# Two of 192 attention tiles change from transposed ("upright") to ordinary scores, about 120 single operations change engine, and the order table is replaced

## The chip, the cores and the metric

The kernel runs on one NeuronCore of one Trainium2 chip. The metric is the device time of one execution in microseconds. TensorE is called PE here (its weight loads PEld), VectorE DVE, ScalarE ACT, GpSimd POOL and SyncE SP; all DMAs of this kernel are issued by SP.

## The reference

Clustered attention, then a softplus feed-forward network:

```python
q_assign = argmax(einsum('bhsd,hcd->bhsc', q_n, c_n), axis=-1)   # 16 centroids per head
k_assign = argmax(einsum('bhsd,hcd->bhsc', k_n, c_n), axis=-1)
mask   = q_assign[:, :, :, None] == k_assign[:, :, None, :]
scores = where(mask, scale * (q @ k.T), -1e9)
attn   = softmax(scores, axis=-1)
x      = (attn @ v).transpose(0, 2, 1, 3).reshape(3072, 512)
out    = softplus(x @ w_in) @ w_out          # w_in 512x2048, w_out 2048x512
```

Batch 4, 8 heads, 768 positions, head width 64. Inputs and output are float32 (the two weights arrive as 64-bit words and are converted on the chip); the kernel splits each operand into a high and a low float16 part, so that a product is two or three float16 matmuls.

## The kernel before

**Tiles and passes.** A tile t is 128 queries of one head. There are 8 passes (4 batches, two halves of the 768 queries each); a pass has 8 heads and 3 tiles per head, so 24 tiles. Tiles 0 to 23 are the first pass, 24 to 47 the second; both belong to batch 0 and use the same keys. Two neighbouring tiles make a pair: pair 17 is tiles 34 and 35.

**The two ways to compute scores.** An ordinary tile (`scores`, L971 to L1041) has 4 matmuls (L991) that give 128 queries by 768 keys, a row maximum on DVE (L1007), the exponential on ACT into `p` (L1013), a float16 copy of `p` on ACT (L1022), the rest `p` minus copy on POOL (L1024), both into `phl`, and, once for a pair, a DMA transpose of 24 blocks (`flip`, L303) from `phl` into `pt`, which the second product needs with keys on the partitions. Its second product (`attend`, L1071 to L1073) is 18 float16 matmuls. An upright tile (`upright`, L880 to L969) avoids the transposition: 2 matmuls (L890) for the maximum alone, the maximum on DVE (L902), a PE transpose of it (L909), a copy into an extra row of the queries on ACT (L915), then 12 matmuls (L926, L927) that give the scores already transposed with the maximum subtracted, and the exponential on ACT (L967). Its second product is done in float32 (L1067). The constant `UPRIGHT` lists the upright pairs: 0 to 17, so tiles 0 to 35. For heads with an upright tile, row 64 of the transposed keys is filled by a small DMA (`lift`, L529), and `prep_q` fills row 64 of those query tiles that are not upright by another (L770).

**Around them.** `prep_k`, `prep_q` and `prep_v` load keys, queries and values, split them and transpose them (on PE for the first heads, else by DMA); `nearest` (L533 to L587) finds the centroid of each row with small matmuls and a chain of DVE operations; `prep_weights` converts 32 pieces of the weights (L398 to L408). `ffn1` (L1138 to L1140), `softplus` (L1159 to L1187; its high part is `gh` by an ACT cast L1186, its low part a POOL subtraction L1187) and `ffn2` (L1216 to L1218) compute the network for one pass while the attention of the next is under way. All this overlaps: PE alternates between pieces of `ffn1` and `ffn2` and the attention tiles.

**What sets the order.** Each of these functions is a generator that yields one operation at a time, and the string `PLAN` says whose turn is next, two characters an entry. So each engine's instructions stand in the order that the table gives, and each engine runs its own in that order. An operation has an engine and a planned duration; where the table's planned times leave a gap on PE, `warm` (L273) puts filler matmuls there (L279), which compute nothing. SP's queue is in order as well: a DMA whose source is not ready holds up those behind it.

The lines that decide which pair is upright:

```python
UPRIGHT = (0, 1, ..., 17)                      # L33, shortened here
def is_up(t): return t // 2 in UPRIGHT         # L418
lows = [c for c in range(c12) if not is_up(at + c)]   # prep_q, L765
```

Of the kernel before, what the change touches and what calls it, by code (L numbers as in the profile page):

```python
# [12 lines left out]
AF = mybir.ActivationFunctionType  # L13
# [18 lines left out]
UPRIGHT = (0, 1, 2, 3, 4, 5, 6, 7, 8, 9, 10, 11, 12, 13, 14, 15, 16, 17)  # L32
# [3 lines left out]
QLO_POOL = (1, 4)  # L36
QT1_ACT = (0,)
POOLED = ('q0_0_0', 'q0_0_1')
SPLIT = ()
HI_POOL = ()  # L40
HALVES = (0,)

# [4 lines left out]
    "020306000704d1c3d2000000000000000000000001d3050501d40c0a000006060101d50101d1d106d1d2d2d606d1d2d2010101010101"  # L47
    "d70ac40507c305c4c50a070cd806d7d1d1d1d101d9d2d2d106d2d206d206d1d106d106d2d206d106c601da06dcd1dad2d2080bc70cdb"
    "d101c5d1d1070906c4061fc51fd2d21h1h1f1f08070808d2d21h1h1j1j1f0b0b1fc80b1j1l1l1h1h1j0ac3c4c5c31g1n1j1l1n1i0909"
    "09c51l1j0cc30a0c0509c3080808081p1p1k1n1n1l1l080808c9ca08cb1p1r1r0b0b0bdddd1n1n0b1pc61r1t1r1mc71t0b09090b1t1p"  # L50
    "1o09090bdfc4090909dfdh1p1r1r1tc8c4c51v1vdhdhdh1q1q1q1q1x1t1v1t1q1v1sc9didididjdedi1q1x1z1z1v1x1v1x1uccdg0bcd"
    "1z1z1x21c6c6c7c7c6c61w211z21ca1x23c7c8cac8c71zcb21cc1y23252321caca2120dk0dce1qcf2525c923cdc8cbc9c9cc27272225"
    "2222222323cac8c92927272222250d25292b2b242d272b2926ce27290d0dcdce2d2d292f28ccccce2b292f2hcbcb2f0d2b2d2f2bcccb"
    "2h2j2h2a2dcf2hce2d2ccgcg2f2e0d0d0d0d0dcdcf0dcf0d2j0d2l2jcg2f2ncfcf22chchcicjcd2j2e2e2e2g0d0d0d0d2l2h2h2n2lcg"
    "cg2j2j2n2ichch2n2lci2ech2p2pcgck2kce2l2l2pcicicichclci2n2r2r2pcj2ncjcj2m2t2p0e2rckckck2p2rckcj2ecm2ecjcd2o2r"
    "2r2t2v2v2q2q2q2q2tclcl2t2x2t2v0e0e0e2v2t2qck2q2s2v2x2x2v2xcm2z2z2ucn2q2x312zclclcmcmcmcm312w2z2xcl0e0e0eco2z"
    "33330e0e0e0e0e31312y2zcncncn33310f31cz353533czcpcococo0e33dncncndndn3735cz300f0f37czcq33coco35dodo3732390f0e"
    "0e0e0ecz35cr0hdododocpcq39cz323232323234320e3735dqdq0f3937363b3937cpcpcqcp39cr0fcqcqdqcz3b3b0fcpcrcr393b0f3d"
    "3dczcrcrcsdrdrdr0f0f38cz3b0h0h0f0fdrdr3bcq3d3dczdtdtdt3d0i3d3f3f3aczdsctcscscs3f3h3h3f3fdscz3c3j3j3e0fcscs0g"
    "0i0i3hd03ldud03hctct3jcz3n3hducu0i3e3e3e3h0jduct3l3j3e3eduducz0ict3lcu0gct3ndw3n3pd03rcudw0g0k0gcu3jdwczcz0i"  # L60
    "3p0i0icz3gcz3lcucucv3l3l3n3n3p3tdxdx3rdxcz3pdxdx3p3t3r3v3vd03i3pcz0jdycvcv0icv3tdydy3xcz0kdzd03kcz3m0jcvcvcw"
    "e03r3re03t3t3te03x3v3ze1e1e1e1e00ke03z3x3ocz3q3q3q3q0i0icwcw3zcxczczd0cz410k0ne2e23q0i0i0mcwcw3qe2e2czd0czcw"
    "e241d03x3v3ve3e3e3e4cxcx3x3x3se5e5e5e5cz3ue40gcxcx410ne5cxcze7e70n0n41413z3z0me6d00k0ke70k0k0k0k0k0kd0czd0cz"
    "e9e9e9e9cy3wd0ea0m413q3e0le8e83y0g0g0g0ge9cycy0gcy0gcy0g0g0g0gcy0gd0d0d04042420o42424242d0eb0g0o0l420n0n0n0n"
    "0nd0d00n0n0necec0keb0nd0434343430l0lcz43454545454545cz4747474747edcz4949494949ed49d0eeeeczef4b4b4bedd04d4dd0"
    "0l4fefef4def0oefd04f4b4b4h0l0l0l4h0l4d4d44d0egeg4f4j0l0l0l4jcz464d4h4l4l4hcz4f4f4h48cz4a4hczeh0l0l0l4jeheh4n"
    "4n4lcz4p0p0lcz4ceieiei4n4pcz4e4e4e4e4j4j4l4l4lejeieiejej4pczd0cz4g4e4e4eek4n4nekekcz0p4p4pelekekel4r4r4r4i4p"
    "4t4tczd0elel4t4v4v4r4r4k4x4x4t4t4m4t4vcz4x4z4zczemem514zcz4o0p0p4v4v51emem534q4q4q4qen4x4x4xencz51d0534q4q55"
    "55em4sen534z4zczeo514u5757eoeo0p5551514qczd0eoeo0p0p0pep57cz53534w59590p5555d04y55eqeqeq5b59cz5d0q5b0p0p0p0p"
    "0p0p5057575bczerer52520p0p5d595959er52525252ererczd0czesesesd0545b5b5d525d5dcz565dczetet0q5f5fetcz5f5h5hetcz"  # L70
    "5j0q0q5f5f5h5h5h5j5jcz58cz5a5h5l5ld0eweueueueu5jet5j5c5n5n5l5l5l5e5l5e5e5e5n5e5e5ed05p5p5p0r0qevevd05r0q0q0q"
    "0q0q0q0q5revd05t5g5n5n5t0q0qevd0ex5i5p5p5p5r5v5v5t5r0q0q5r5t5t5v5k5x5x5xcz5m5tczeyey0r0r5z5z5z5vczd0czezey5o"
    "5v5x5xezevcz61615q5qez5q5q0r616363czf0f0f0d05x65655scz5z5z0r5ucz0t0uezez5q63676161610r0rd06569f1f1f1f15w0r67"
    "0rcz69656563635y65czf1d067f2f20u0u0u0sf2cz696b6b0r0t0t5qczf4f4f4f36d0w6dcz67676b60czf5f5f569696262626962cz6f"
    "6fcz0r0r0r6b6b64czf6f6f6f6f66d0s0s0sf36d6d666d6fd0czf4f46hf7f76h6hf8f86h6hd00u0u0u0ud06j6j6jf868d0f9f90u0u0u"
    "6f6fcz6a6hcz0w0w6l6lfafafa62d06l0u0ufafa625q626n6n6nczfbfb6j6j6pczfcfcfc6l6l6ccz6e6e6e6pczfdfd6ed00s0s0s0s0s"
# [1238 lines left out]
```

## Time and profile before

| | us |
|---|---|
| median of 3 runs | 828.7 (827.96 to 829.2) |
| the profiled execution | 827.06 |
| its span in the profile | 825.2 |
| PE busy | 810.4 (98%) |
| ACT, POOL, DVE busy | 556.0, 507.6, 478.4 |
| clock granted to PE | full speed in each of the 40 slices |

The span runs from the first to the last instruction of the program; 1.86 us of the profiled execution lie outside of it. The profiled execution is 1.64 us under the median of the timed ones. Durations in the profile that belong to one matmul are longer than the time it keeps PE, since matmuls overlap: what one costs is read from the start of one to the start of the next.

### The profile page before, as it was taken

Reading aid. Unit: us, or ns where it says so; the run is one execution under the profiler, and the core shown is the slowest. Engines: PE = TensorE matmul, PEld = TensorE weight load, DVE = VectorE, ACT = ScalarE, POOL = GpSimd, SP = SyncE. Lnnn points to the kernel's source line nnn. Section 1 sums busy time; section 2 is a strip of 40 time slices with the busy share of each in tenths; the row PEclk is TensorE's granted clock in tenths of the full one; section 3 lists DMA queues with packets and bytes.
Section 4 is the critical chain, followed back from the end, with each engine's and each line's share of the span. In section 5 each row is a group of like instructions: output and inputs, shape, how many; then the busy total and the mean of one; then the engine's idle time right before and its main releaser. Section 6 shows DMA issues by size and latency. Waiting matters only on the chain.

```text
span 825.2 us, 19179 instructions
## 1 busy us (share of the span) xinstructions
PE 810.4 (98%) x7941; PEld 526.8 (64%) x7941; DVE 478.4 (58%) x861; ACT 556.0 (67%) x858; POOL 507.6 (62%) x361
## 2 busy tenths in 40 slices
PE   8899999999999999999999999999999999999998
PEld 8899886655666666656666666566666655655554
DVE  7788787676655856665674546667555453322111
ACT  6687788865787788658678677767767666623230
POOL 4743457884788778767686685756775656621210
PEclk9999999999999999999999999999999999999999
DMA  9987759999999999989989999999898776620001
GB/s 251 221 193 161 190 157 212 204 212 188 185 181 174 186 214 193 209 181 176 187 166 183 177 182 180 212 199 186 154 155 169 136 129 122 114 64 13 26 1 39
DMA packets 389815, 133.68 MB, mean 162 GB/s; under 512 B 367072, under 2 KB 382688, under 8 KB 389728
## 3 DMA queue, kind: packets, MB, share of 16 engines
q1 hardware_dynamic: 389728, 132.46, 80.7%
q8 instruction: 62, 1.02, 0.5%
q14 instruction: 25, 0.20, 0.1%
HBM read 35.68 MB, written 6.29 MB: 51 GB/s over the span
## 4 chain that ended last, share of the span: by engine, by line
PE 63%; issue 8%; DMA 5%; ACT 2%; DVE 2%; POOL 2%; POOLq 0%; DVEq 0%; ACTq 0%
PE s L991 10%; PE h L1138 7%; PE h L1139 7%; PE h L1140 7%; PE o L1218 7%; PE o L1216 7%; PE o L1217 7%; DMA pt<-phl 5%; PE mbank L1071 3%; PE mbank L1073 3%; PE mbank L1072 3%; POOL gh L1187 1%; ACT p L1013 1%; ACT phl L1022 0%; DVE fg L1171 0%
## 5 line engine op out<-in xcount | busy, mean ns | idle before, releaser
L1024 POOL TENSOR_TENSOR phl<-p,phl 128x768 f16<-128x768 f32 x156 | 255.9, 1652 | 114.0 <-ACT phl L1022 77.4
L1007 DVE TENSOR_REDUCE negm<-s 128x1 f32<-128x768 f32 x156 | 148.7, 954 | 91.6 <-PE s L991 89.9
L1013 ACT ACTIVATE p<-s,negm 128x768 f32<-128x768 f32 x156 | 139.4, 896 | 52.3 <-DVE negm L1007 46.8
L1138 PE MATMUL h<-xT,wi 128*128 128x384 f16 x512 | 166.7, 325 | 1.1 <-DVE fg L1171 1.1
L1140 PE MATMUL h<-xT,wi 128*128 128x384 f16 x512 | 166.8, 326 | 0.0
L1139 PE MATMUL h<-xT,wi 128*128 128x384 f16 x512 | 166.7, 326 | 0.0
L1187 POOL TENSOR_TENSOR gh<-fg,gh 128x768 f16<-128x768 f32 x64 | 105.2, 1646 | 86.9 <-ACT gh L1186 86.6
L1216 PE MATMUL o<-wo,gh 128*128 128x512 f16 x376 | 142.4, 379 | 0.4 <-DVE ot L1261 0.4
L1218 PE MATMUL o<-wo,gh 128*128 128x512 f16 x376 | 142.5, 379 | 0.0
L1217 PE MATMUL o<-wo,gh 128*128 128x512 f16 x376 | 142.4, 379 | 0.0
L1022 ACT CAST phl<-p 128x768 f16<-128x768 f32 x156 | 127.3, 828 | 19.7 <-DMA pt<-phl 17.5
L1171 DVE SCALAR_TENSOR_TENSOR fg<-fa,h 128x384 f32<-128x384 f32 x128 | 70.3, 550 | 119.7 <-ACT fa L1160 108.8
L1159 ACT ACTIVATE fa<-h 128x384 f32<-128x384 f32 x128 | 62.4, 487 | 111.2 <-PE h L1140 111.1
L991 PE MATMUL s<-kt,qt 128*128 128x384 f16 x624 | 126.9, 326 | 0.1
L1071 PE MATMUL mbank<-vb,pt 128*128 128x65 f16 x936 | 101.2, 192 | 3.0 <-DMA pt<-phl 3.0
L1072 PE MATMUL mbank<-vb,pt 128*128 128x64 f16 x936 | 101.3, 192 | 0.0
L1073 PE MATMUL mbank<-vb,pt 128*128 128x65 f16 x936 | 100.9, 194 | 0.0
L1071 PEld LDWEIGHTS <-pt 128*128 128x128 f16 x936 | 86.9, 98 | 17.0 <-DMA pt<-phl 5.1
L1072 PEld LDWEIGHTS <-pt 128*128 128x128 f16 x936 | 86.3, 97 | 11.6
L1073 PEld LDWEIGHTS <-pt 128*128 128x128 f16 x936 | 86.5, 97 | 0.0
L991 PEld LDWEIGHTS <-qt 128*128 128x128 f16 x624 | 57.6, 98 | 38.2 <-issue 0.6
L1140 PEld LDWEIGHTS <-wi 128*128 128x128 f16 x512 | 50.0, 98 | 33.2
(164 smaller groups left out, 1279.4 us busy)
## 6 DMA issues: line engine op xcount, KB each, us to landing
wo<-in_moe_w_in_dram SPq DMA_DIRECT2D x16, 512.0 KB, 6.0
wo<-in_moe_w_out_dram SPq DMA_DIRECT2D x14, 512.0 KB, 4.5
out_dram<-ot SPq DMA_DIRECT2D x23, 256.0 KB, 3.0
rawk<-in_k_dram SPq DMA_DIRECT2D x15, 384.0 KB, 4.2
rawq<-in_q_dram SPq DMA_DIRECT2D x15, 384.0 KB, 4.1
rawv<-in_v_dram SPq DMA_DIRECT2D x12, 384.0 KB, 4.5
rawv<-in_v_dram SPq DMA_DIRECT2D x8, 192.0 KB, 6.0
pt<-phl SPq DMA_TRANSPOSE x78, 6.1
```

What stands on the lines that cost most here:

```text
L991: nc.tensor.matmul(st[:, j, :SH], qt[:, s, i], kt[:, s, NT // 2 * j : NT // 2 * (j + 1)], start=(s == 0), stop=(s == 1),)
L1007: yield op("DVE", 950, lambda: nc.vector.tensor_reduce(negm, st[:, :, :SH], AX.XY, ALU.max, negate=True))
L1024: "POOL", 1640, lambda: nc.gpsimd.tensor_tensor(phl[:, u, 1], p32, phl[:, u, 0], ALU.subtract), shared=True
L1071: nc.tensor.matmul(av, pt[:, 0, c], vb[:, c, D : 2 * D + 1], start=(c == 0), stop=False)
L1072: nc.tensor.matmul(av[:, :D], pt[:, 0, c], vb[:, c, :D], start=False, stop=False)
L1073: nc.tensor.matmul(av, pt[:, 1, c], vb[:, c, D : 2 * D + 1], start=False, stop=(c == NT - 1))
L1138: nc.tensor.matmul(hp, w[0], x[0], start=(c == 0), stop=False)
L1139: nc.tensor.matmul(hp, w[0], x[1], start=False, stop=False)
L1140: nc.tensor.matmul(hp, w[1], x[0], start=False, stop=(c == NP - 1))
L1216: nc.tensor.matmul(po, g[0], wo[:, f, 0, 0], start=(f == f0), stop=False)
L1217: nc.tensor.matmul(po, g[0], wo[:, f, 0, 1], start=False, stop=False)
L1218: nc.tensor.matmul(po, g[1], wo[:, f, 0, 0], start=False, stop=(f == f0 + NF // 2 - 1))
```

## The change

`UPRIGHT` loses its last entry, 17. Tiles 34 and 35 are then ordinary. `prep_q` for heads 0 to 3 of the second pass gets a small DMA that fills row 64 of these two query tiles.

A new tuple `SWAPPED` names single operations that run on the other of two engines. Each such place in the code now has two engines with a planned duration for each:

```diff
+    def either(key, first, second, emit, **opt):
+        now, other = (second, first) if key in SWAPPED else (first, second)
+        if "shared" not in opt or now[0] == "ACT":
+            opt["shared"] = now[0] == "POOL"
+        return op(now[0], now[1], lambda: emit(engines[now[0]]), alt=other, key=key, **opt)
+    def cast(key, ns, slow, dst, src):
...
+        return either(key, ("ACT", ns), ("POOL", slow), emit)
...
-UPRIGHT = (0, 1, 2, 3, 4, 5, 6, 7, 8, 9, 10, 11, 12, 13, 14, 15, 16, 17)
+UPRIGHT = (0, 1, 2, 3, 4, 5, 6, 7, 8, 9, 10, 11, 12, 13, 14, 15, 16)
...
-        yield op("ACT", 830, lambda: nc.scalar.copy(phl[:, u, 0], p32))
-        yield op(
-            "POOL", 1640, lambda: nc.gpsimd.tensor_tensor(phl[:, u, 1], p32, phl[:, u, 0], ALU.subtract), shared=True
+        yield cast(f"ph{t}", 830, 1290, phl[:, u, 0], p32)
+        yield either(
+            f"p{t}",
+            ("POOL", 1640),
+            ("DVE", 950),
+            lambda e: e.tensor_tensor(phl[:, u, 1], p32, phl[:, u, 0], ALU.subtract),
+            shared=True,
...
-        eng, n_e, e = last
-        yield op(eng, n_e, lambda: e.tensor_scalar(other, sim, 1.0, MASK, ALU.subtract, ALU.mult), **here)
+        def mark(e):
+            if e is nc.scalar:
+                e.activation(other, sim, AF.Copy, bias=-MASK, scale=MASK)
+            else:
+                e.tensor_scalar(other, sim, 1.0, MASK, ALU.subtract, ALU.mult)
+
+        yield either(f"zk{n}", last[:2], ("ACT", 310), mark, **here)
```

Counted in `SWAPPED`, by kind:

- POOL to DVE: 23 subtractions of attention tiles (`p34, p35, p37, p39, p40, p41, p43, p45, p46, p61, p62, p64, p67, p82, p84, p85, p88, p90, p100, p102, p133, p190, p191`), 13 of the network (`g0_6, g0_7, g1_1, g1_7, g2_2, g2_5, g2_7, g6_5, g7_2` and `g7_4` to `g7_7`), 5 of the weights, 5 of `x`, 3 of keys (`k4, k8, k16`), 3 of values (`v8, v16, v20`), and 4 products of the later queries (`m`).
- ACT to POOL: 40 float32 to float16 copies: 12 of attention tiles (`ph`), 10 of the weights, 8 of the network, 7 of `x`, 2 of keys, 1 of values.
- DVE to ACT: 9 marks of key clusters (`zk`), 4 of query clusters (`zq`).
- ACT to DVE: 5 copies of the maximum (`u1, u12, u17, u22, u23`).
- At the start: the copies out of PSUM `kT0_0_0` and `qT1_0` go from ACT to DVE, `kT0_2_1`, `kT1_0_1`, `kT1_2_1` and `qT1_1` from DVE to ACT; the product `m0_0_0` goes from DVE to POOL and `m0_0_1` from POOL to DVE; the second half of the first keys' subtraction (`k0_1`) goes from DVE to POOL.

`PLAN` is replaced. Both tables have 3304 entries: `scores` of tile 34 has 5 instead of 6, `prep_q` of heads 0 to 3 in the second pass 18 instead of 17. Read as PE's order, the table after has the same phases in the same order, with neighbours exchanged; the scores of tiles 34 and 35 come between `ffn1` pieces 2 and 4 of the first pass, and the DMA transpose of this pair between weight loads 25 and 26. The first query load stands behind the first weight load instead of ahead of it, and the fill of row 64 of the first keys stands 13th on SP's queue instead of 16th. From `ffn1` piece 15 of the seventh pass to the end PE's order is the same in both.

Two waits (`acc`) are made explicit in `store` and `last_store`; they name what the order gave before.

## Rows read from the trace of the kernel before

**Rows 1.** The page's span and its first part: busy time, share of the span and instructions of each engine.

```profile
span 825.2 us, 19179 instructions
PE 810.4 (98%) x7941; PEld 526.8 (64%) x7941; DVE 478.4 (58%) x861; ACT 556.0 (67%) x858; POOL 507.6 (62%) x361
```

**Rows 2.** Busy time by stretch. Columns: the stretch and its length in us, then busy us and instructions of each engine, the clock granted to PE as a share of full speed, the busy share of the DMA engines, GB/s.

```profile
0.00:20.00 20.00, 17.20 (x298) 16.09 (x299) 14.29 (x66) 12.12 (x20) 8.81 (x23) 1.00 0.93 250
20.00:100.00 80.00, 76.02 (x917) 70.53 (x914) 66.10 (x118) 60.15 (x106) 40.61 (x38) 1.00 0.80 188
100.00:200.00 100.00, 97.20 (x913) 65.63 (x910) 75.17 (x130) 73.78 (x120) 67.48 (x50) 1.00 0.94 201
200.00:700.00 500.00, 498.01 (x5029) 307.74 (x5028) 294.74 (x499) 367.16 (x542) 359.56 (x233) 1.00 0.94 176
700.00:826.00 126.00, 121.96 (x798) 66.84 (x796) 28.06 (x49) 42.76 (x73) 31.13 (x20) 1.00 0.19 44
```

**Rows 3.** The filler matmuls of L279 alone, by stretch, in the same columns (PE and PEld only).

```profile
0.00:20.00 20.00, 10.78 (x153) 10.03 (x154) 1.00 0.93 250
20.00:100.00 80.00, 4.40 (x66) 3.71 (x62) 1.00 0.80 188
100.00:200.00 100.00, 0.53 (x7) 0.46 (x7) 1.00 0.94 201
```

**Rows 4.** PE's waits over the whole span: who waited for what, us in total, times, longest. These are three of eleven lines.

```profile
PE mbank L1071 <- DMA pt<-phl: 3.0, 4, 1.2
PE turned L909 <- ACT qt L915: 1.2, 1, 1.2
PE h L1138 <- DVE fg L1171: 1.1, 2, 0.6
```

**Rows 5.** PE's timeline around an upright tile: start, duration (of several, from the first start to the last end), instruction. The 12 of L926 and L927 run from 28.08 to 28.75.

```profile
26.41 1.50 PE L1067 MATMUL mbank<-rawv,ptf 128*128 128x65 f32 x12
27.75 0.49 PE L890 MATMUL m<-kt,qt 128*128 128x384 f16 x2
28.08 0.22 PE L926 MATMUL u<-qt,kt 128*128 128x128 f16 x1
...
28.75 0.28 PE L909 MATMUL turned<-eye,negu 128*65 128x128 f32 x1
28.86 0.33 PE L1067 MATMUL mbank<-rawv,ptf 128*128 128x65 f32 x2
```

**Rows 6.** PE's timeline around ordinary tiles: the 4 of L991 and what starts behind them; then the first of the 18 matmuls of a second product, and what starts behind the last of them.

```profile
210.15 0.81 PE L991 MATMUL s<-kt,qt 128*128 128x384 f16 x4
210.80 0.19 PE L1071 MATMUL mbank<-vb,pt 128*128 128x65 f16 x1
...
214.27 0.19 PE L1071 MATMUL mbank<-vb,pt 128*128 128x65 f16 x1
...
214.82 0.81 PE L991 MATMUL s<-kt,qt 128*128 128x384 f16 x4
```

**Rows 7.** SP's timeline: the stretch from 123.80, where the table after puts the new transpose, and the last attention transpose of the second pass.

```profile
123.80 0.47 SPq L298 DMA_DIRECT2D wo<-in_moe_w_out_dram  x1
127.00 2.15 SPq L303 DMA_TRANSPOSE kt<-kn  x1
...
130.78 0.50 SPq L298 DMA_DIRECT2D wo<-in_moe_w_out_dram  x1
134.60 1.43 SPq L303 DMA_TRANSPOSE kt<-kn  x1
...
180.62 4.76 SPq L303 DMA_TRANSPOSE pt<-phl  x1
```

**Rows 8.** PE's timeline, the longest wait in 183 to 198 us (in brackets: idle time before, and what ended it), and the piece of the critical chain (start, duration, what) that ends at it.

```profile
188.87 0.20 PE L1071 MATMUL mbank<-vb,pt 128*128 128x65 f16 x1 [1.16 <-DMA pt<-phl]
...
180.62 8.20 DMA pt<-phl
```

**Rows 9.** DVE's timeline just ahead of PE's two waits for `fg` (start, duration, instruction), and POOL's beside the second.

```profile
140.61 2.40 DVE L735 SCALAR_TENSOR_TENSOR qn<-rawq,qn 128x768 f16<-128x768 f32 x1
...
143.53 0.54 DVE L1171 SCALAR_TENSOR_TENSOR fg<-fa,h 128x384 f32<-128x384 f32 x1
...
152.30 1.65 DVE L581 TENSOR_TENSOR eq_k<-eq_k,tab 128x192 f16<-128x192 f16 x1
...
152.05 1.78 POOL L465 TENSOR_TENSOR vb<-rawv,vb 128x768 f16<-128x768 f32 x1
```

**Rows 10.** The nearest operation that DVE does in the form of the moved subtractions (count: min/median/max in ns, first and last start), and the groups of the subtractions and casts of attention tiles on POOL and ACT (count | busy us, mean ns | idle before, and what ended it).

```profile
L735 DVE SCALAR_TENSOR_TENSOR qn<-rawq,qn x14: 946/1037/2401, 62.3 to 627.9; 128x768 f16<-128x768 f32 x14
L1024 POOL TENSOR_TENSOR phl<-p,phl 128x768 f16<-128x768 f32 x156 | 255.9, 1652 | 114.0 <-ACT phl L1022 77.4 <-issue 29.5 <-DVE al L691 1.6
L1022 ACT CAST phl<-p 128x768 f16<-128x768 f32 x156 | 127.3, 828 | 19.7 <-DMA pt<-phl 17.5
```

**Rows 11.** The start: the last DVE result of the first queries, the first score matmuls on PE, and POOL's two products of the second two heads' queries.

```profile
16.81 0.24 DVE L827 TENSOR_REDUCE aq<-qn 128x6 f16<-128x96 f16 x1
...
20.39 0.82 PE L890 MATMUL m<-kt,qt 128*128 128x384 f16 x4
...
18.85 0.83 POOL L835 TENSOR_TENSOR qn<-qn,aq 128x384 f16<-128x384 f16 x1 [1.68 <-DVE qn L837]
19.63 0.40 POOL L837 TENSOR_TENSOR qn<-qn,aq 128x6 f16<-128x6 f16 x1
```

More of the change, by code (lines that the diff above doesn't have):

```diff
@@ L52 @@
[L52 to L56, printed above, removed]
@@ L286, in op, with emit @@
         return ("op", eng, ns, emit, opt)
+    engines = {"DVE": nc.vector, "ACT": nc.scalar, "POOL": nc.gpsimd}
+    def either(key, first, second, emit, **opt):
[4 more added lines that the diff above has]
+    def cast(key, ns, slow, dst, src):
+        def emit(e):
+            (e.copy if e is nc.scalar else e.tensor_copy)(dst, src)
+        return either(key, ("ACT", ns), ("POOL", slow), emit)
     def wait(*name):
@@ L406, in prep_weights @@
         )
-        yield op("ACT", 655, lambda: nc.scalar.copy(part[:, 0], val))
-        yield op("POOL", 1160, lambda: nc.gpsimd.tensor_tensor(part[:, 1], val, part[:, 0], ALU.subtract), shared=True)
+        yield cast(f"wh{step}", 655, 890, part[:, 0], val)
+        yield either(
+            f"w{step}",
+            ("POOL", 1160),
+            ("DVE", 640),
+            lambda e: e.tensor_tensor(part[:, 1], val, part[:, 0], ALU.subtract),
+            shared=True,
+        )
         od.set(("wr", step))
@@ L473, in tile_cluster_attention__then__softplus_ffn, with evict, emit @@
     vkey, kkey, qkey = {}, {}, {}
+    def evict(key, first, second, dst, src):
+        def emit(e):
+            (e.copy if e is nc.scalar else e.tensor_copy)(dst, src)
+        return either(key, first, second, emit)
     def turn(dst, src, name: str, on_chip: bool, ready=(None, None), done=(None, None)):
@@ L518, in first_half @@
     def first_half(dst, ps, name, done, hk):
-        yield op("ACT", 820, lambda: nc.scalar.copy(dst[:, :NT], ps))
+        yield evict(f"{name}_0", ("ACT", 820), ("DVE", 560), dst[:, :NT], ps)
         od.set(("half", name))
@@ L726, in prep_q @@
         if pi == 0:
-            yield op("ACT", 850, lambda: nc.scalar.copy(n1[:, :, D:], qf))
-            eng, ns, e = ("POOL", 1640, nc.gpsimd) if n in QLO_POOL else ("DVE", 950, nc.vector)
-            yield op(eng, ns, lambda: e.tensor_tensor(n1[:, :, :D], qf, n1[:, :, D:], ALU.subtract), shared=True)
+            yield cast(f"qh{sfx}", 850, 1290, n1[:, :, D:], qf)
+            yield either(
+                f"q{sfx}",
+                ("POOL", 1640),
+                ("DVE", 950),
+                lambda e: e.tensor_tensor(n1[:, :, :D], qf, n1[:, :, D:], ALU.subtract),
+                shared=True,
+            )
         else:
@@ L820, in first_q @@
         )
[L821 to L822 removed]
+        yield either(f"zq0_0_{u}", last[:2], ("ACT", 220), mark_queries(n2[:, part, ROWS : ROWS + NCL], sim), **here)
         yield wait("al", 2 * u)
@@ L850, in turn_part @@
         yield op("PE", 350, emit)
-        yield op(*copy, lambda e=copy[0]: (nc.scalar.copy if e == "ACT" else nc.vector.tensor_copy)(dst, ps))
+        yield evict(name, ("ACT", 800), ("DVE", 560), dst, ps)
         od.set(sk)
@@ L1185, in softplus @@
         if not two:
-            yield op("ACT", 830, lambda: nc.scalar.copy(gh[:, 0], g))
-        yield op("POOL", 1640, lambda: nc.gpsimd.tensor_tensor(gh[:, 1], g, gh[:, 0], ALU.subtract), shared=True)
+            yield cast(f"gh{pi}_{fp}", 830, 1290, gh[:, 0], g)
+        yield either(
+            f"g{pi}_{fp}",
+            ("POOL", 1640),
+            ("DVE", 950),
+            lambda e: e.tensor_tensor(gh[:, 1], g, gh[:, 0], ALU.subtract),
+            shared=True,
+        )
         od.set(fk)
```

256 lines of the change are left out of this document (149 added, 107 removed).

## The prediction

> **What bounds the kernel now.** I read the page's first part, then busy time by stretch, then PE's waits, then the timelines of what the change touches. PE is busy for 810.4 of 825.2 us [rows 1], at the full granted clock in every stretch [rows 2]. From 200 to 700 us it is busy for 498.0 of 500 us, while ACT and POOL have over 130 us free and DVE over 200. There only less PE work gains time, and a faster POOL or ACT gains nothing. The time that PE loses lies earlier. In 20 to 100 us it is idle for 4.0 us and runs 4.4 us of fillers, in 100 to 200 us it is idle for 2.8 us and runs 0.5 us of fillers [rows 2, 3]; the first 20 us hold 10.8 us of fillers while the first keys and queries are prepared. The named waits are few: attention transposes (3.0 us in all), one copy of a maximum (1.2 us), two softplus results of DVE (1.1 us) [rows 4]. So I count PE work first, then what can happen to some 8 to 11 us of waits and fillers ahead of 200 us.
>
> **PE work of the two tiles.** Start to start, an upright tile costs 27.75 - 26.41 = 1.34 us for the float32 second product, 28.08 - 27.75 = 0.33 for the maximum's matmuls, 28.75 - 28.08 = 0.67 for the 12 matmuls and 28.86 - 28.75 = 0.11 for the transpose, 2.45 us [rows 5]. An ordinary tile costs 210.80 - 210.15 = 0.65 for the scores and 214.82 - 214.27 = 0.55 for the second product, 1.20 us [rows 6]. Two tiles: 2 x 1.25 = 2.5 us less. These instructions run in 100 to 135 us, where PE is the busiest engine, so I take all of it; how much stays is the first rival's question.
>
> **What the two tiles add elsewhere.** One transpose of 24 blocks: SP issues such a one in up to 4.8 us, and one took 8.2 us to land [rows 7, 8]. Its place in the new table is behind the weight load of 123.80. SP then stands idle for 2.7 us (124.27 to 127.00), so up to 2.1 us of it push the following issues, and the next idle stretch, 131.28 to 134.60, is longer than that [rows 7]. Cost 0 while these gaps are there, 2 us on every later transpose of the second pass if they close. The small fill of row 64 is one more issue of about half a microsecond (the neighbouring plain DMAs take 0.47 and 0.50 us [rows 7]), at a place ahead of it with idle SP: 0. Two ACT casts of 0.83 us [rows 10] stand against ACT's 26 free us in that stretch [rows 2]: 0.
>
> **Subtractions from POOL to DVE.** Nine of the 23 moved ones (tiles 34 to 46) fall in 100 to 200 us, and with them, by their places in the tables, one of keys, one of values, two of the network and two of the weights. On POOL one takes 1.65 us; the nearest DVE row has the same shape, minimum 0.95, median 1.04, longest 2.40 us [rows 10]. For the 13 of full size DVE gets 13 x 1.04 = 13.5 us (12.4 to 31.2), so it goes from 75.2 to about 89 us of 100 [rows 2], less some 2 us for five cluster marks that go to ACT. POOL loses 13 x 1.65 = 21.5 of 67.5 us and gets back at most 1.65 us for each of some seven casts. The gain is that the low parts, and so the transposes, are ready earlier: the transpose that PE waited 1.16 us for was issued at 180.62 and landed at 188.82 [rows 8], with POOL loaded at 67%. The cost is a queue: behind a subtraction on DVE wait the row maxima (L1007) that release the next scores, and the softplus results that release PE's two `ffn1` buffers. Rows 9 show what that costs now: DVE's 2.40 us operation at 140.61 and its 1.65 us one at 152.30 (beside POOL's 1.78 us one) each stand ahead of an `fg`, and both `fg` are the ones PE waited for, 1.1 us in all [rows 4]. I take a net of -0.5 us for 20 to 200 us, bounds -4 (half of the 7 to 11 us of waits and fillers goes) and +5 (below, second rival).
>
> The row first: the same two-input operation takes 0.95 us or 2.40 us, the long one while DVE had nothing else to wait for in its own row [rows 9, 10]. The Trainium skill ("SBUF — State Buffer", Who interferes with whom) gives a rule that speaks against the move: a DVE instruction with two SBUF inputs contends with a GpSimd instruction that reads SBUF, and the second to issue is blocked for the whole of the first. The stretched rows agree with it; by that rule each moved subtraction could be held for one POOL operation, which is the price of the second rival.
>
> **Casts from ACT to POOL.** No row has a 768-wide cast on POOL. Bounds: ACT's 0.83 us and POOL's two-input 1.65 us [rows 10]; I take the upper, since POOL's row is the nearer one. Most of the 40 lie after 200 us, where POOL has 140 us free [rows 2] and the planned lead before use is several us: 0 on the path, and 0 to 1 us if one delays a transpose that PE waits for.
>
> **The start.** Now the first maximum's matmul starts at 20.39, 3.34 us after the last DVE result of the first queries (16.81 + 0.24) [rows 11]. After, that product runs on POOL: 0.83 + 0.40 us as POOL's rows show it for the other half [rows 11], and the copy behind it goes from ACT to DVE. Marks and three of the PSUM copies leave DVE, which is busy for 14.3 of the first 20 us [rows 2]; the fill that the first tile waits for is issued three loads earlier, but the first query load stands behind a weight load. I take -0.5 us, bounds -1.5 to +0.5.
>
> **The tail** from 700 us on loses nothing to POOL or DVE now (both are under 32 us busy of 126 [rows 2]), and PE's order at the end is unchanged: 0.
>
> **Sum.** -2.5 - 0.5 - 0.5 = -3.5 us. On the profiled execution that is 825.2 - 3.5 = 821.7 us of span and 823.6 us in all; on the median of the runs, which lies 1.64 us over the profiled execution, 828.7 - 3.5 = **825.2 us**. With the bounds of the start and of the small terms, and the waits from -2 to +1.3, its own range is 822.7 to 827.0.
>
> **Rivals.**
> 1. *The freed PE time turns into waiting.* All of tiles 36 to 47 and the first scores of the third pass hang on transposes that SP issues in order, and one has been added. If SP's gaps [rows 7] close, PE finishes its upright tiles 2.5 us earlier and waits that much longer at the second products of the second pass, where it waits today [rows 8]. For: the DMA engines are busy for 0.94 of 100 to 200 us [rows 2]. Against: the new transpose stands where SP idles, and nine subtractions ahead of these transposes get shorter. Only the start's 0.5 us would stay: 828.2 us.
> 2. *DVE becomes the bound in 100 to 200 us.* Place: `fg` and the row maxima behind the moved subtractions. Price: PE lost 1.1 us behind two stretched operations [rows 4, 9], 0.55 us each; at worst a stretched one is 2.40 - 0.95 = 1.45 us longer [rows 10]. If half of the 13 cost PE 0.75 us, a value between these, that is 4.9 us: 828.7 - 2.5 - 0.5 + 4.9 = 830.6 us, slower. It decides from about six such waits on (6 x 0.75 = 4.5 us against 3.0 us gained). Against it: DVE still has 10 us free there, and POOL, which stretches it, does a fifth to a third less.
> 3. *The waits go as well.* POOL's relief and the shorter maximum chain take away half of the waits and fillers between 20 and 200 us, 4 us: 828.7 - 2.5 - 0.5 - 4 = 821.7 us.
> 4. *The change doesn't do what it says*: if PE's records showed no fewer float32 second products, nothing would change in PE's work; the diff leaves no room for that, and it gets no chance of its own.
>
> **How the numbers follow.** Forecast 0.61, rival 1 0.16, rival 2 0.15, rival 3 0.08. A measurement of this kernel can tell about 0.2%, or 1.7 us, from no change, so faster means under 827.0 and slower over 830.4. Faster: 0.58 of the forecast (a little of its upper end is lost to same) and rival 3, 0.66; same: rival 1 and that rest, 0.19; slower: rival 2, 0.15. The range goes from 822.0, which leaves out half of rival 3, to 829.0, which takes in rival 1 and leaves out rival 2: 0.8.
>
> **What would show it.** L1067 with 408 instead of 432 records, L926 with 204 instead of 216, L991 with 632 instead of 624: the PE work. A first L890 ahead of 20.4 us: the start. PE's waits for `fg` and for `pt` over 100 to 200 us: if their sum is under 3 us, the forecast stands; if the waits for `pt` grow by 2 us, rival 1; if those for `fg` or a maximum grow by 4 us, rival 2, with long DVE subtractions ahead of them. A new kind of wait after 200 us that costs over 2 us would make the forecast wrong for a reason that I don't name here.

## The result, and the profile after

The changed kernel took 837.4 us (median of 4 runs, 835.4 to 839.4) against 829.0 us before: ratio 1.0099, 95% interval 1.0081 to 1.0117. Six more runs of it later gave 830.9 to 838.8 us, median 836.0. The forecast was 825.2 us with a range of 822.0 to 829.0: wrong in size and in sign.

The page of the profiled execution (835.44 us), span and PE, against [rows 1]:

```profile
span 833.7 us, 19105 instructions
PE 812.7 (97%) x7901; PEld 527.4 (63%) x7901; DVE 524.4 (63%) x906; ACT 535.8 (64%) x828; POOL 469.5 (56%) x348
```

Busy time by stretch, columns as in [rows 2]:

```profile
30.00:36.00 6.00, 4.39 (x72) 3.99 (x69) 4.31 (x9) 4.30 (x9) 5.87 (x6) 1.00 1.03 261
36.00:37.00 1.00, 1.00 (x7) 0.82 (x6) 0.49 (x2) 0.75 (x2) 0.00 (x0) 0.60 0.90 239
37.00:46.00 9.00, 9.00 (x76) 8.63 (x75) 5.00 (x15) 2.88 (x6) 2.27 (x2) 0.50 0.81 167
46.00:47.00 1.00, 1.00 (x11) 1.00 (x9) 0.20 (x2) 0.48 (x1) 0.94 (x1) 0.78 0.00 0
...
60.00:100.00 40.00, 36.38 (x411) 33.47 (x409) 34.47 (x60) 26.58 (x46) 20.19 (x19) 1.00 0.58 160
100.00:200.00 100.00, 95.10 (x931) 65.06 (x930) 89.09 (x144) 71.80 (x120) 55.22 (x43) 1.00 0.94 202
200.00:300.00 100.00, 96.25 (x996) 59.91 (x995) 74.52 (x112) 71.91 (x106) 66.79 (x46) 1.00 1.00 181
```

Two of these stretches in the kernel before (100 to 200 us stands in [rows 2]):

```profile
60.00:100.00 40.00, 38.68 (x451) 36.42 (x449) 32.00 (x54) 30.47 (x55) 16.96 (x17) 1.00 0.68 169
200.00:300.00 100.00, 100.00 (x1054) 63.24 (x1053) 65.04 (x107) 80.67 (x120) 79.12 (x52) 1.00 1.01 180
```

Two things are new. From 36 to 46 us PE is busy without a gap, but at a granted clock of 0.50, the lower of its two levels (1.2 GHz); 76 matmuls run in 9 us. Before, the clock was 1.00 in every stretch [rows 2]. And in 60 to 300 us PE is idle for 3.62 + 4.90 + 3.75 = 12.3 us; before it was 1.32 + 2.80 + 0.00 = 4.1 us.

PE's waits over the span (total, times, longest), which answer to [rows 4]:

```profile
PE s L1064 <- ACT p L1086: 4.6, 5, 1.6
PE turned L976 <- ACT qt L982: 2.5, 2, 1.6
PE h L1219 <- DVE fg L1252: 1.8, 4, 1.1
...
PE u L996 <- DVE negu L969: 1.5, 2, 1.3
PE h L1219 <- DVE eq_k L603: 1.4, 1, 1.4
```

The waits for attention transposes fell from 3.0 to 0.9 us. In their place stand waits for exponentials of ACT (the first line, which was no line of its own before) and for row maxima, gates and cluster marks of DVE. A gate here is a softplus result, `fg` or `gh`; a cluster mark is a result of `nearest` (`eq_k` and what follows from it).

What came ahead of the fall of the clock is a stand of PE, that is, a time in which it waits and does nothing: PE's timeline (the two transpositions, with the stand between them) and ACT's beside it.

```profile
33.95 0.30 PE L976 MATMUL turned<-eye,negu 128*65 128x128 f32 x1
35.86 0.32 PE L976 MATMUL turned<-eye,negu 128*65 128x128 f32 x1 [1.61 <-ACT qt L982]
```

```profile
33.60 0.81 ACT L1040 ACTIVATE ptf<-u 128x768 f32<-128x768 f32 x1 [0.34 <-PE u L997]
34.31 1.21 ACT L412 ACTIVATE wi<-wo 128x512 f32<-128x512 f32 x2
35.54 0.27 ACT L982 ACTIVATE qt<-turned 1x128 f16<-1x128 f32 x1
```

The second transposition waits for ACT's copy, which its row names. The copy takes 0.27 us, but the new table puts two weight steps (1.21 us) ahead of it on ACT. The kernel before waits for such a copy of ACT too, at about the same time but ahead of another tile's transposition, for 1.2 us [rows 4].

To split the difference I took for each line's matmuls their lower-quartile step from start to start times their count (the work), and everything PE took beyond these steps (the rest). Before: 799.1 us of work and 21.1 us of rest. After: 795.0 and 33.9 us. So the work fell by 4.1 us (2.5 us of the two tiles, 1.6 us of 30 fillers fewer), and the rest grew by 12.8 us, where the forecast had it fall by 1.0.

### The profile page after: what moved, and what is told of

The parts are those of the page before. It is cut to its first block, busy times and chain, and to the rows that moved or that the text cites. A ratio compares the mean times of both kernels' runs of the same rounds, so it can differ in the third digit from the quotient of the medians.

```text
span 833.7 us, 19105 instructions
## 1 busy us (share of the span) xinstructions
PE 812.7 (97%) x7901; PEld 527.4 (63%) x7901; DVE 524.4 (63%) x906; ACT 535.8 (64%) x828; POOL 469.5 (56%) x348
## 4 chain that ended last, share of the span: by engine, by line
PE 66%; DMA 4%; DVE 4%; POOL 2%; ACT 2%; issue 2%; SPq 0%; ACTq 0%; POOLq 0%; DVEq 0%
PE s L1064 9%; PE o L1303 8%; PE o L1305 8%; PE o L1304 8%; PE h L1219 8%; PE h L1221 8%; PE h L1220 8%; DMA pt<-phl 4%; PE mbank L1150 3%; PE mbank L1148 3%; PE mbank L1149 3%; POOL phl L1100 1%; DVE negm L1080 1%; ACT p L1086 1%; ACT phl L298 1%
## 5 line engine op out<-in xcount | busy, mean ns | idle before, releaser
L1100 POOL TENSOR_TENSOR phl<-p,phl 128x768 f16<-128x768 f32 x135 | 225.5, 1678 | 117.4 <-ACT phl L298 89.2
L1086 ACT ACTIVATE p<-s,negm 128x768 f32<-128x768 f32 x158 | 141.4, 897 | 63.4 <-DVE negm L1080 57.4
L298 ACT CAST phl<-p 128x768 f16<-128x768 f32 x146 | 120.1, 829 | 21.8 <-DMA pt<-phl 19.0
L1272 POOL TENSOR_TENSOR gh<-fg,gh 128x768 f16<-128x768 f32 x51 | 86.4, 1696 | 60.5 <-ACT gh L298 58.7
L1148 PE MATMUL mbank<-vb,pt 128*128 128x65 f16 x948 | 102.3, 192 | 0.9 <-DMA pt<-phl 0.9
L1150 PE MATMUL mbank<-vb,pt 128*128 128x65 f16 x948 | 102.0, 194 | 0.0
L1148 PEld LDWEIGHTS <-pt 128*128 128x128 f16 x948 | 88.0, 98 | 14.2 <-DMA pt<-phl 2.4
L1149 PEld LDWEIGHTS <-pt 128*128 128x128 f16 x948 | 87.4, 97 | 11.8
L1150 PEld LDWEIGHTS <-pt 128*128 128x128 f16 x948 | 87.6, 97 | 0.0
```

What stands on the lines that cost most here:

```text
L1100: lambda e: e.tensor_tensor(phl[:, u, 1], p32, phl[:, u, 0], ALU.subtract),
L1148: nc.tensor.matmul(av, pt[:, 0, c], vb[:, c, D : 2 * D + 1], start=(c == 0), stop=False)
L1149: nc.tensor.matmul(av[:, :D], pt[:, 0, c], vb[:, c, :D], start=False, stop=False)
L1150: nc.tensor.matmul(av, pt[:, 1, c], vb[:, c, D : 2 * D + 1], start=False, stop=(c == NT - 1))
```

## The experiments

Medians below are of 4 to 12 runs each, with the kernel before beside them on the same chip. Over all experiments that kernel ran 135 times with its clock listed. In 105 of them its mean granted clock was 0.999 or more (median 828.7 us), in 29 it was 0.992 to 0.996 (median 831.9 us), in one 0.998. Line numbers differ by a few between kernels.

### The clock

**Fill the stand at 34 us.** 30 fillers ahead of tile 5's transposition, in the changed kernel.

```diff
+        def turn_max():
+            if t == 5:
+                for _ in range(30):
+                    nc.tensor.matmul(idle, eye, ones[:, :WARM], start=True, stop=True)
+            nc.tensor.transpose(out=ps[:ROWS], in_=negm.to_broadcast([P, ROWS]), identity=eye32)
```

> The changed kernel with 30 more filler matmuls on TensorE ahead of the fifth upright tile's transposition, where TensorE stood for 1.8 us at 34.1 us before its granted clock fell to 0.50 for 10.2 us; nothing else is touched. Theory A (the fall of the clock follows from that stand, and is some 5 of the 8.5 us lost): the clock stays at 1.00 through 30 to 50 us and the time is 832 to 833 us. Theory B (the fall comes from something else, or what it costs is made up later by waits): the clock falls all the same, or the time stays at 836 to 838 us.

Measured 829.9 us (ratio to before 1.0003, 0.9986 to 1.0020), clock 1.00 in 12 of 12 runs. PE's timeline at the stand, and the busy time by stretch behind it:

```profile
34.16 1.74 PE L976 MATMUL mbank<-ones,eye 128*128 128x120 f16 x30
35.88 0.32 PE L977 MATMUL turned<-eye,negu 128*65 128x128 f32 x1
```

```profile
37.00:46.00 9.00, 8.39 (x111) 7.93 (x110) 8.33 (x21) 5.75 (x11) 5.73 (x7) 1.00 0.75 175
```

The transposition starts at the same time as in the changed kernel (35.88 against 35.86 us), so the fillers gain nothing by themselves; what they gain comes after. In 37 to 46 us PE now runs 111 matmuls where it ran 76. The clock did what theory A says, and the gain was larger than the 5 us that it named.

**Take the stand away by order.** The copy goes ahead of the two weight steps in the table; no added filler.

```diff
-...1r1nc6c71r050a...
+...1r1n1rc6c7050a...
```

> The changed kernel with one step moved in its order table and no further filler: the copy of the seventh upright tile's shift goes ahead of the two weight steps that stood between it and the exponential on ScalarE, so that the next transposition need not wait 1.8 us for it at 34 us (fillers held to the changed kernel's own 192). Theory A (the fall of the clock follows that stand): the stand falls to some 0.6 us, the clock stays at 1.00 through 30 to 50 us, and the time is 829 to 830 us. Theory B (the fall has another cause, and 30 fillers more only happen to prevent it): 836 to 838 us.

831.4 us (1.0018, 0.9998 to 1.0038), and no run below 0.999; the stand at 34 us fell to 0.46 us. This is a second way to the same end, without fillers: theory A stands, theory B falls, though the time is 1.4 us above what A named.

**The changed kernel again.**

> The changed kernel itself, once more, with more runs. If the one fall of the clock at 36 us is all that the first of these experiments took away: a median of 834.5 to 836 us, every run at a mean clock of 0.994 or 0.995. If the clock falls longer or a second time in most executions: a median of 836.5 to 838 us, runs at 0.992 among them, and a second stretch under 1.00 in the profile.

Median 836.0 us of 6 runs: four at 0.992 to 0.994 (835.9 to 838.8 us) and two at 1.00 (830.9 and 834.5 us). Neither half of the expectation had that. The profiled execution is one of the two: span 829.1 us, the same stand as ever, and no fall behind it:

```profile
35.67 0.32 PE L976 MATMUL turned<-eye,negu 128*65 128x128 f32 x1 [1.61 <-ACT qt L982]
```

```profile
37.00:46.00 9.00, 8.39 (x111) 7.93 (x110) 8.33 (x20) 5.56 (x10) 5.94 (x7) 1.00 0.63 157
```

So the stand does not force the fall; it makes it likely. In all, 8 of 10 runs of the changed kernel had a mean clock of 0.992 to 0.994, and none of the 24 runs with the stand filled or taken away, and nothing else changed, had (all at 0.999 or 1.00). Length alone doesn't decide either: the changed kernel has another stand of 1.61 us, at 163 us, and no fall behind it in the profile. In the rest as defined above, this execution has 29.2 us against 33.9: one fall costs 4.7 us. What decides in a single execution the traces don't show, and I don't know why the medians of the changed kernel lie further (6.1 to 7.5 us) above the 829.9 us with the stand filled than one fall costs in the profile.

**The same fillers in the kernel before.** The edit of the first run, in the kernel before.

> The kernel before with 30 more filler matmuls on TensorE ahead of the fifth upright tile's transposition, and nothing else. Of 17 timed runs of the kernel before, 13 had a mean granted clock of 0.999 or 1.000 (826.9 to 830.2 us) and 4 had 0.994 to 0.996 (831.8 to 834.7 us). Theory A (the kernel before stands at the same place for 1.2 us, and its clock falls there too in some runs): with the fillers every run has a clock of 1.00 and lies between 826 and 831 us, median 828.5 us. Theory B (the falls have another place or cause): some runs still show 0.996 and 832 us.

827.9 us (0.9988, 0.9968 to 1.0008), and two of 12 runs still at 0.996. The edit missed its place: in this kernel tile 5's transposition comes one ahead of the one that waits, so the fillers ran first, and the wait of 1.24 us stands behind them:

```profile
33.18 1.74 PE L909 MATMUL mbank<-ones,eye 128*128 128x120 f16 x30
38.05 0.32 PE L910 MATMUL turned<-eye,negu 128*65 128x128 f32 x1 [1.24 <-ACT qt L917]
```

The run shows only that the edit costs nothing there. Whether the falls of the kernel before come from this stand was not tested.

### The parts of the change, one by one

**Engines back, engines alone, tiles alone.** One part undone or done, with the kernel's own planner left to place fillers.

```diff
-SWAPPED = ('g0_6', 'g0_7', ..., 'zq8_2')
+SWAPPED = ('k0_1', 'm0_0_0', 'qT1_1', 'q0_0_0')
```

> The changed kernel with its order table and its two ordinary tiles, but every single operation back on the engine it had before (casts on ScalarE, scale subtractions and the others on GpSimd). Theory C (the moved operations crowd VectorE and make row maxima late, some 6 us of waits between 60 and 300 us): those waits go, VectorE falls by some 23 us of busy time between 100 and 300 us, and the time falls to 829 to 833 us. Theory D (the order table is written for these engines, so the waits come from the order, and the engines alone do no harm): the time rises to 840 us or more, since ScalarE now holds the casts that the order puts close together.

> The kernel before, with its order table and its upright tiles, but the single operations on the engines of the changed kernel. Theory C (crowding of VectorE by itself): slower than before by 4 to 8 us, 833 to 837 us, with new waits for row maxima. Theory D (it is the new order that costs): within 2 us of before, 827 to 831 us. [...]

> The kernel before with the two tiles ordinary and nothing else moved: its engines, and its order table with only those two tiles' entries put anew. By the sum of the prediction for this part alone, 2 x 1.25 us of TensorE work: 826.5 us. If the freed TensorE time turns into waits or fillers instead: 828 to 830 us. Theory E (the ordinary tiles bring late transpositions, and are themselves part of the loss): 831 us or more.

866.5, 878.8 and 841.5 us. These tell less than was hoped: with another pairing of order and engines the planner's model sees PE waiting and puts fillers there. The first and the third stayed within theory D and theory E, the second was far slower than either of its theories. The filler group of the first of them (after: x192, 14.2 us):

```profile
L277 PE MATMUL mbank<-ones,eye 128*128 128x120 f16 x966 | 61.0, 220 | 2.4 <-DVE ones L247 1.5 <-DVE x L1173 0.9
```

The third has its use for the clock. Its early order is that of the kernel before, and PE waits the same 1.24 us at the same place; in its profile the clock fell behind it, in that of the kernel before it did not:

```profile
36.49 0.32 PE L909 MATMUL turned<-eye,negu 128*65 128x128 f32 x1 [1.24 <-ACT qt L915]
```

```profile
37.00:46.00 9.00, 9.00 (x85) 8.73 (x85) 5.42 (x13) 3.50 (x7) 2.62 (x3) 0.62 0.62 124
```

**The same three with the fillers held** in number and place, and the 30 fillers of the first run.

```diff
-                self.warm(start - self.free[eng])
+                self.warm(FILLS.get(self.turn, 0))
+                self.turn += 1
```

> The changed kernel (order table, tiles) with every single operation on the engine it had before, as in the run of the same name ahead of this one, but with the filler matmuls held to the changed kernel's own 192 in their own places (the kernel's planner had put in 966 of them, 61 us, for these engines), and the 30 more ahead of the fifth upright tile. Theory C (the moved operations crowd VectorE): without the 47 us of needless fillers the time is 826 to 829 us, under the 829.9 us of the changed kernel with the 30 fillers. Theory D (order and engines belong together; the planner was right that TensorE would wait there): the waits show as real ones in the place of fillers, mostly between 100 and 400 us, and the time is 845 us or more.

> The kernel before (order table, tiles) with the single operations on the changed kernel's engines, filler matmuls held to the kernel before's own 222 in their own places, and the 30 more ahead of the fifth upright tile. Theory C (crowding of VectorE by itself): 832 to 836 us, with new waits for row maxima between 100 and 300 us. Theory D (order and engines belong together): 845 us or more, with waits in many places. If neither order nor engines matter by themselves: 828 to 830 us.

> The kernel before with the two tiles ordinary, its own engines and its order table with only those two tiles' entries put anew, filler matmuls held to the kernel before's own 222, and the 30 more ahead of the fifth upright tile. By the prediction's sum for this part alone, 2 x 1.25 us off the 828.6 us of the kernel before without a fall of the clock: 826 us. If the freed time comes back as waits ahead of the two tiles' own transposed products: 828 to 829 us. If the 478 fillers of the run before this one stood where TensorE would have waited anyway: 835 us or more.

870.7, 861.7 and 838.5 us. For the first the planner had been right: without its fillers real waits stand there. The second gained 17 us and the third 3, so a part of the fillers there had been needless, but most of the loss stays. With the engines put back (first run) the longest groups are

```profile
PE s L1064 <- ACT p L1086: 8.0, 7, 3.4
PE mbank L1148 <- DMA pt<-phl: 5.1, 4, 2.9
PE turned L975 <- DVE negu L967: 3.6, 4, 1.7
```

and the clock falls in several stretches as well (mean 0.975 to 0.986 in the six runs). Theory D holds: order and engines belong together, and neither can be had alone. The two tiles by themselves cost time in my own re-placing of their entries (PE busy for 14.8 of the 20 us from 120 to 140 us); another placing may do better, so that number is no price of the tiles.

**Single groups back** (30 fillers, the others held; 829.9 us is the mark).

```diff
-SWAPPED = (all)
+SWAPPED = (all without p34 ... p46 | without the 40 casts | without the 18 of x and g)
```

> The changed kernel with the 30 fillers of the first run (829.9 us there, no fall of the clock), fillers otherwise held to its own 192, and the nine probability subtractions that it moved to VectorE between 100 and 200 us (tiles 34, 35, 37, 39, 40, 41, 43, 45, 46) back on GpSimd. Theory C (these nine, 0.95 us each, push row maxima and gates back on VectorE and so make the waits of 1.2 to 1.6 us at 119, 145 and 158 us): VectorE falls by 8.5 us in that window, those waits shrink, and the time is 827 to 828 us. Theory D (the order is written for these engines: nine more subtractions of 1.67 us on GpSimd make the transposed probabilities late): waits for them return, and the time is 831 to 836 us.

830.3 us: no gain and no loss, so neither theory has the time. DVE's busy time in 100 to 200 us fell from 88.2 to 82.1 us and PE's idle time there from 5.3 to 4.9 us; the waits for `eq_k`, the gate and the exponentials stay. The nine subtractions are not what makes them.

> The same kernel (30 fillers, the others held) with the 40 casts that the change moved to GpSimd back on ScalarE. If the casts' move was worth nothing, as the prediction has it: 829 to 831 us. Theory D (ScalarE then does 0.82 us more, 40 times, ahead of exponentials and of the copies that transpositions wait for, in an order that does not allow for it): 834 us or more, with new waits for ScalarE's exponentials and copies.

855.8 us, 26 us more. The move of the casts, which the prediction took at nothing, carries the new order: without it exponentials and row maxima come late in many places (waits of scores for ACT's exponentials 7.0 us, the longest 3.3 us). A part of the 26 us is the clock, which fell in all five runs (mean 0.986 to 0.992); in the profiled execution I estimate it at 7 us at most, 0.8% of 851 us.

> The same kernel as the first of this call (30 fillers, the others held) with the 5 subtractions of normalised outputs and the 13 of gates that the change moved to VectorE back on GpSimd; the probability subtractions stay on VectorE. Theory C: the wait of 0.6 us at 237 us behind a stretched subtraction of 2.00 us goes, and others with it: 828 to 829.5 us. Theory D: GpSimd's queue grows by 26 us in all, mostly late in the second pass: 831 to 835 us, with waits of the second feed-forward product for gates.

831.4 us: inside theory D's range, at its lower end. The waits that D named are not there: none of the second feed-forward product for gates is among the 17 longest.

### The order

**Six places.** Steps that PE waits for go ahead of steps that nobody waits for; no operation changes engine. The diff shows the table at 60, 76, 81, 119 and 145 us; at 158 us the row maximum of tile 43 (3t) moves ahead of the subtractions of tiles 41 and 40, and its exponential ahead of a weight step (cv).

```diff
-...2222222729...
+...2922222227...
-...2e2e0d2e...
+...2e2e2e0d...
-...cg2l2l...
+...2l2lcg...
-...cqcpcqcpdqdqdq35...
+...cqdqdqdqcpcqcp35...
-...cucucu0g3lct3r3jcu0i0i0i...
+...0i0i0icucucu0g3lct3r3jcu...
```

> The changed kernel with the 30 fillers of the first run (829.9 us there), fillers otherwise held to its own 192, and six places of its order table put in another order, no operation on another engine and none more or less: at 60, 76, 81, 119, 145 and 158 us the step that TensorE waits for (a row maximum, a normalised output, a copy on ScalarE, a gate, a cluster mark, a row maximum with its exponential) goes ahead of steps that nobody waits for (weight shifts, a cast, a copy of q, two subtractions). Theory F (the waits come from the order of the table on VectorE and ScalarE, not from which engine has the single operations): the six waits of 1.51, 1.21, 1.10, 1.23, 1.55 and 1.57 us fall to under 0.6 us each, and the time falls by 4 to 6 us to 824 to 826 us. Theory G (TensorE is only late by what another engine is late over the whole stretch, so the time is lost again at the next place): the waits move on, and the time stays at 828 to 831 us.

> The same six places, and the 30 fillers replaced by the reordering on ScalarE at 34 us of the run before last (831.4 us there). Theory F: 825 to 827 us, at a clock of 1.00 in 30 to 50 us. Theory G: 829 to 832 us.

828.0 us (0.9984, 0.9965 to 1.0002) and 830.3 us: 1.9 and 1.1 us better than without the six, not the 4 to 6 expected. The waits at 60 and 145 us and the one for the gate at 119 us went, and those at 76 and 81 us fell to 0.5 and 0.4 us; PE's idle time in 60 to 100 us fell from 3.6 to 1.3 us. But at 152 and 159 us two gates became late in their turn (PE idle for 1.9 and 1.5 us): theory F there, theory G here.

**Ten places.** At 151 us a gate (dy) and a row maximum (3r) move ahead of cluster marks (0i) and a weight step (ct), at 159 us a gate (dz) ahead of weight steps (cv), at 203 us an exponential (43) ahead of the cast of v (0o), and at 260 us, in the diff, a row maximum (59) ahead of cluster marks (0p).

```diff
-...0p0p57cz53534w59594y...
+...57cz53534w59590p0p4y...
```

> The run before last (six places, 30 fillers, 828.0 us) with four more places of the order changed and nothing else: at 151 us a gate and a row maximum go ahead of the cluster marks' two steps and a weight's subtraction; at 159 us a gate's two steps go ahead of a weight's shift and or; at 203 us an exponential goes ahead of the cast of v, which waits for its load; at 260 us a row maximum goes ahead of two steps of the cluster marks. Theory F (order alone): the waits of 2.0, 1.6, 1.0 and 0.75 us fall to under 0.5 us each, and the time falls by 3 to 4.5 us to 823.5 to 825 us, which is what the prediction's sum gave for the change. Theory G (VectorE, busy for 88 of the 100 us from 100 to 200 us, is short there): new waits of the same size stand elsewhere in 140 to 200 us, and the time stays at 827 to 829 us.

827.8 us (0.9991, 0.9971 to 1.0010). In 200 to 300 us PE's idle time fell from 1.7 us with six places to 0.4 us, but in 100 to 200 us it rose from 5.4 to 7.7 us, with a gate of the network and transposes late:

```profile
PE mbank L1148 <- DMA pt<-phl: 3.4, 3, 1.9
PE h L1219 <- DVE gh L1256: 1.9, 1, 1.9
```

The clock has a part in it again: the 1.9 us wait for the transpose ended at 133 us, and the profile shows a fall behind it.

```profile
133.00:137.00 4.00, 3.58 (x42) 2.81 (x43) 1.30 (x4) 2.46 (x5) 3.57 (x3) 0.57 1.13 267
```

Four of the 11 runs had a mean clock of 0.998 (830.1 to 831.9 us); the median of the other seven is 827.4 us.

**Ten places and less work for DVE; seven places.** The second leaves out the edits at 151, 158 and 159 us.

> The run with ten places changed (827.8 us), and the nine probability subtractions of 100 to 200 us back on GpSimd, as in the run that moved them back alone. Theory G' (VectorE is short of time in 100 to 200 us): with 8.5 us less of its work, TensorE's idle time in that stretch falls from 7.7 us to under 4.5 us, and the time to 824 to 825.5 us. Theory H (the stretch is tight on every engine; GpSimd takes 1.67 us where VectorE took 0.95): the waits turn into waits for transposed probabilities, idle time stays at 6 us or more and the time at 827 to 829 us.

> The changed kernel with the 30 fillers and seven places in another order: those at 60, 76, 81, 119 and 145 us and those at 203 and 260 us, but not those at 151 and 159 us. If the edits at 151 and 159 us made the new waits: idle time in 100 to 200 us of under 4.5 us and 825 to 826.5 us. If VectorE is short there: one wait of 1.5 us at 158 us, as in the changed kernel, and others, 5 us idle or more, and 826.5 to 828 us.

831.1 us (1.0030, 1.0015 to 1.0045), idle time in 100 to 200 us 8.1 us: theory H in the waits (4.6 us for transposes), with a time 2 us above what it named. Eight of the 12 runs were at a clock of 0.995 to 0.998; the other four have a median of 830.1 us. And 827.1 us (0.9968, 0.9950 to 0.9987) with the seven places, the one version that measured faster than the kernel before; the idle time is as its first expectation had it, the time as its second. Its stretches:

```profile
60.00:100.00 40.00, 38.67 (x436) 35.89 (x434) 37.24 (x64) 28.67 (x50) 18.69 (x19) 1.00 0.63 161
100.00:200.00 100.00, 95.85 (x904) 62.77 (x904) 86.06 (x143) 70.26 (x116) 54.09 (x42) 1.00 0.96 207
200.00:300.00 100.00, 99.58 (x1050) 63.06 (x1049) 75.16 (x116) 77.35 (x115) 72.90 (x51) 1.00 1.03 185
```

The same stretches of the first run of all (30 fillers, no place changed):

```profile
60.00:100.00 40.00, 36.38 (x410) 33.72 (x409) 35.52 (x61) 26.72 (x47) 17.66 (x18) 1.00 0.56 150
100.00:200.00 100.00, 94.67 (x907) 63.03 (x905) 88.19 (x144) 69.96 (x116) 54.33 (x42) 1.00 0.95 202
200.00:300.00 100.00, 97.93 (x1022) 61.52 (x1021) 75.47 (x111) 75.30 (x111) 69.08 (x48) 1.00 1.03 184
```

PE is idle for 1.33 + 4.15 + 0.42 = 5.9 us with the seven places, for 3.62 + 5.33 + 2.07 = 11.0 us without. How one place works, in DVE's timeline at the gate of 119 us, first in the run with the 30 fillers alone, then with the seven places:

```profile
116.91 1.81 DVE L414 TENSOR_SCALAR wo<-wo 128x512 int32<-128x512 int32 x2 [0.29 <-ACT wo L412]
118.64 1.28 DVE L418 SCALAR_TENSOR_TENSOR wo<-wo 128x512 int32<-128x512 int32 x2
119.85 0.54 DVE L1254 SCALAR_TENSOR_TENSOR fg<-fa,h 128x384 f32<-128x384 f32 x1
```

```profile
116.07 0.75 DVE L412 TENSOR_SCALAR wo<-wo 128x512 int32<-128x512 int32 x1 [0.29 <-ACT wo L410]
117.00 0.56 DVE L1252 SCALAR_TENSOR_TENSOR fg<-fa,h 128x384 f32<-128x384 f32 x1 [0.18 <-ACT fa L1241]
117.47 0.42 DVE L412 TENSOR_SCALAR wo<-wo 128x512 int32<-128x512 int32 x1
```

Four weight steps, 3 us, stood ahead of a gate for which PE was idle 1.07 us. Now three of them follow it, and the wait for the gate is gone; a wait of 0.5 us for a cluster mark has come behind it.

## Why the prediction was wrong

**PE work of the two tiles: right.** The counts are those foretold (float32 second products 432 to 408, the upright tiles' matmuls 216 to 204):

```profile
L1144 PE MATMUL mbank<-rawv,ptf 128*128 128x65 f32 x408 | 52.7, 281 | 0.0
L996 PE MATMUL u<-qt,kt 128*128 128x128 f16 x204 | 27.6, 224 | 1.6 <-DVE negu L969 1.5
```

By steps and counts that is the 2.5 us of the sum. The new transpose cost nothing that shows: the waits for transposes went from 3.0 to 0.9 us, so rival 1 is out.

**"At the full granted clock in every stretch": the first step that failed.** The prediction read this off one execution and carried it into the changed kernel as if it were a property of the work; no term of its sum is for the clock. The kernel before itself had a lower clock in 29 of 135 runs. The view of PE's waits that the prediction quoted had the wait of 1.2 us for ACT's copy in it. It asked what that wait costs, not what a longer one does to the clock. The new table has one of 1.6 us there, and 8 of 10 executions had a lowered mean clock; in the profiled one that is some 10 us at 0.50. Price: 4.7 us in the profiled executions; between the medians (837.4 or 836.0 against 829.9 and 831.4 us) 4.6 to 7.5 us.

**Net -0.5 us for 20 to 200 us of waits, and nothing after 200 us: the second.** In the fall-free run of the first experiment PE is idle for 11.0 us between 60 and 300 us, where the kernel before had 4.1. By the prediction's own stretches, 20 to 200 us has 9.8 us idle against 6.8, so 3.0 us the wrong way (and that with one stand of 1.6 us filled): inside the bound of +5 that it worked out, but above the +1.3 that it put into its range without a reason. In 200 to 300 us it is 2.1 us, where it had 0. The upper end of its range is also added up short: with +0.5 us for the start and +1.3 for the waits it is 828.0, not 827.0.

Rival 2 had the engine and the kind of wait right in part: row maxima and gates are late on DVE, which is busy for 89 of 100 us, as worked out; but the longest line is the wait for ACT's exponentials, and the cause was another. Nine of the thirteen subtractions it counted, put back, gave nothing (830.3 us). That its 830.6 us lies near the 829.9 us without the fall is luck. The sign that the prediction set for itself misled as well: after the change the waits for `fg` (1.8 us) and for `pt` (0.9 us) stay under its 3 us, at which the forecast was to stand. A moved subtraction on DVE took 1.06 us in the mean, near the 1.04 us taken, and the longest of the 23 took 1.75 us:

```profile
L1100 DVE TENSOR_TENSOR phl<-p,phl 128x768 f16<-128x768 f32 x23 | 24.2, 1056 | 2.0 <-ACT phl L298 2.0
L298 POOL CAST phl<-p 128x768 f16<-128x768 f32 x12 | 10.2, 852 | 10.6 <-ACT p L1086 4.4 <-DMA pt<-phl 4.4 <-ACT fa L1241 1.8
```

What made a good part of the waits is the order: seven places of it, changed, with no operation on another engine, gave back 5.1 us of idle time in 60 to 300 us and 2.8 us of time between the medians (4.1 us between the profiled executions). The prediction read the new table for where moved operations lie, and for SP's queue, but not for what stands ahead of what on ACT and DVE at the places where PE would need the result next. Between 100 and 200 us order alone does not give all back (4.2 to 7.7 us idle in every version, 2.8 in the kernel before); that DVE is short there was argued, but taking the nine subtractions from it (88.2 to 82.1 us busy in one pair of runs, 80.3 to 76.9 in the other) did not help, so the cause of this remainder stays open.

**Casts from ACT to POOL, 0: the time taken was too long, the weight too small.** Those of attention tiles took 0.85 us there, near the lower of the two bounds and not the 1.65 us taken. But the new order needs them: undone in it, 26 us are lost, the falls of the clock among them. What the move alone is worth no run shows.

**Start -0.5 us, tail 0: too small to matter.** The first maximum's matmul starts at 20.18 us, 0.2 us earlier.

On the sum: 829.9 us without the fall, less 2.8 us by seven places, is 827.1 us; the forecast of 825.2 us lay 1.9 us lower still. One wait of 1.9 us for a gate at 152 us is the longest that is left in that version.

## What to carry to other kernels

A short stand of the bounding engine can cost more than itself (here 1.6 us idle, and 4.7 us behind it): before calling a wait cheap, look at what the granted clock does behind it, in more than one execution. When a written-out order is replaced, read the new one on each helper engine at every place where the bounding engine needs a result, and count what stands ahead of it; an operation that nobody waits for, one place too early, can cost up to its whole duration (here 3 us of weight steps, 1.07 us of PE). And don't price parts of such a change alone: order and engines that were planned together lost 26 to 50 us when one was put back without the other, some of it by falls of the clock.

## What the runs showed of the hardware that was not expected

- Behind the same stand of PE of 1.61 us the clock fell to 0.50 in one profiled execution of the changed kernel and not in another; behind the same stand of 1.24 us it fell in the profile of the kernel with the two tiles alone and not in that of the kernel before. In the changed kernel the fall lasted 10 us, with PE busy for 9.00 of 9.00 us inside it, and cost 4.7 us.
- A 768-wide cast of attention tiles on POOL takes 0.85 us, hardly more than on ACT (0.83 us [rows 10]), while POOL's subtraction of the same width takes 1.68 us.
